# Retention and a maxout layer in one kernel: the values of a tile's four blocks put into one insertion

## The chip, the cores and the metric

The kernel runs on one core of a Trainium2 chip. The metric is the device time of one execution in microseconds (us); lower is better. The tensor engine is called PE here, VectorE is DVE, ScalarE is ACT, GpSimd is POOL, and SP is the engine that issues nearly all transfers.

## The reference

```python
batch, n_heads, seq, head_dim = (8, 8, 576, 64)
# retention
scores = scale * np.matmul(q, k.transpose(0, 1, 3, 2))
gamma = 1.0 - 2.0 ** (-5.0 - np.arange(H, dtype=np.float32))
rel = pos[:, None] - pos[None, :]
Dmat = np.where(rel >= 0, gamma[:, None, None] ** rel[None, :, :], 0.0)
attn = np.matmul(scores * Dmat[None], v)
x = attn.transpose(0, 2, 1, 3).reshape(B * S, H * D)        # 4608 x 512
# maxout layer, w1, w2, w3: 512 x 768, w_out: 768 x 512
h = np.maximum(np.maximum(x @ w1, x @ w2), x @ w3)
out = h @ w_out
```

All is float32 on the chip; the weights come as 64-bit floats, which the kernel turns into float32 itself.

## The kernel before

**Tiles and chunks.** The 4608 tokens are nine tiles (0 to 8) of 512 tokens; a tile is four chunks (blocks) of 128, called a, b, c, d in `steps`. A chunk of the retention part goes through five steps: `load` and `load_blocks` issue its transfers, `transposes` turns q and k, `decay` scales v (on ACT, one head at a time, handed out by `scale`), `scores` multiplies k by q and makes the state of the next 64 tokens, `values` makes the retention output, which DVE scales into the tile `xT`.

From chunk 8 on (`BY_CHUNKS`) scores and values work on pieces of 64 tokens, in the four 64x64 quarters of PE: `chunk_scores` (L323 scores `sk`, L326 states `kv`) and `chunk_values` (L440, masked scores by v; L447, q by the state). After the scores DVE masks them (L330, `m`) and one or two `keep_chunk` steps add the new state to the old (L338, into a buffer `s`); where the state belongs to the next chunk POOL scales it (L340). After the values DVE makes two outputs for each pair of chunks (`xT<-o,gq`, shown at L209), and with the last pair 13 sums of columns of x (`sums_of_x`).

**The layer.** `ffn(t)` is the layer of tile t. From tile 1 on, the three products x @ w are made by a scheme with fewer multiplications on sums of blocks: `up` has 20 products for each of three groups of hidden columns, each of two matmuls of 256 columns (L816), with copies from PSUM on ACT (L801) and joins on DVE (L804). `downs` (tiles 2 to 8) makes the output by 20 products more (L661) into chains E, G, I, H, C, F, D, with copies on ACT (L650) and sums on DVE (L484). One of these sums, `u = C + k7` after product 15, reads the PSUM bank of chain C, on which product 19 goes on adding. Tile 1 uses another scheme for the output (`downs_seven`), tile 0 plain products.

**How the two are woven.** While the layer of tile t runs, the retention part of tile t + 1 is made in between, at twelve places: `steps(t + 1)` is a list of what is done at each, and `ffn(t)` yields at these places. Places 0 to 8 lie one ninth of the 120 matmuls of `up` apart (after matmul 14, 27, 40, 54, 67, 80, 94 and 107), place 9 at their end, 10 behind the fourth product of `downs`, 11 behind the tenth. What is put in between on PE at a place is called an insertion.

DVE steps and loads are not done at their place but put in a queue, `urgent`, by `soon`. Within `up`, one is taken every four matmuls (one more when over six wait); `scores` and `values` empty the queue first. In the last products two are taken per product. Other DVE sums (`chores`) take the remaining turns. ACT scalings are taken one per three matmuls, and all at the next scores. [...]

**Buffers.** `part` tiles (11) hold copies, states, transposed q of the first chunks and other short-lived data. Transposed q has the tag m1 (3 buffers), transposed k the tag kT (2), masked scores the tag m0 (2). States share 4 buffers (tag s), v 4, `xT` 2. The PSUM pool `ps_r` has four banks: scores of two chunks take all four, the values of a pair take two.

## Time and profile before

| what | value |
| --- | --- |
| median of three runs | 744.47 us (743.42 to 744.48) |
| the profiled execution | 744.55 us, its span 742.0 us |
| PE / PE weight loads / DVE / ACT / POOL busy | 735.4 / 607.4 / 578.2 / 336.2 / 36.6 us |
| scores, 64x64 (L323 and L326), records | 896 and 784 |
| values, 64x64 (L440 and L447), records | 896 and 800 |
| outputs `xT<-o,gq`, 128x512 (L209) | 28, 683 ns each |
| transposes on DVE, 128x512 (L209), k and q | 26 of 704 ns, 26 of 692 ns |
| 64-partition state sums (L338) / masks (L330) | 43 of 689 ns / 28 of 687 ns |
| granted PE clock | 1.00 |

The profile comes from one execution. Starts and durations are in us from the start of its span. PE's matmuls overlap one another, so their durations add up to more than the time they take; starts tell the rate. One float32 matmul of the program leaves two records.

### The profile page before, as it was taken

To read this page: it belongs to the slowest core of one execution; us is meant where nothing else is said; L and a number is where in the kernel's file an instruction comes from. 1 tells how busy PE (TensorE), PEld (TensorE's weight loads), DVE (VectorE), ACT (ScalarE), POOL (GpSimd) and SP (SyncE) were. 2 spreads that over 40 slices of the span, in tenths; PEclk is the share of its full clock that TensorE was granted. 3 is DMA by queue.
4 is the path that set the end of the run, shared out by engine and by line. 5 is a ranking of instruction groups with operands and counts; after the bars stand their busy time and mean duration, and the time that the engine had idled before them with its cause. 6 is when DMAs were issued, how large, how long until landed. Compare 5 with 4: busy or idle time off the path is not lost.

```text
span 742.0 us, 16834 instructions
## 1 busy us (share of the span) xinstructions
PE 735.4 (99%) x6716; PEld 607.4 (82%) x6716; DVE 578.2 (78%) x1061; ACT 336.2 (45%) x693; POOL 36.6 (5%) x42
## 2 busy tenths in 40 slices
PE   8999999999999999999999999999999999999998
PEld 6645546888888888888888888888888888888887
DVE  4998899999886895698668876788768956893676
ACT  4764533454255434544355425543455255424441
POOL 2000000022000100000000001000100010000000
PEclk9999999999999999999999999999999999999999
DMA  9996842505242505241424243232514150000001
GB/s 217 241 244 142 227 94 77 96 14 96 66 84 43 103 31 103 41 82 44 109 55 71 45 100 73 45 71 49 122 25 92 42 114 18 1 31 29 0 1 57
DMA packets 230493, 59.30 MB, mean 80 GB/s; under 512 B 211216, under 2 KB 229136, under 8 KB 230416
## 3 DMA queue, kind: packets, MB, share of 16 engines
q1 hardware_dynamic: 229152, 57.98, 36.1%
q8 instruction: 52, 0.85, 0.5%
q10 hardware_dynamic: 1264, 0.27, 0.2%
q14 instruction: 25, 0.20, 0.1%
HBM read 48.76 MB, written 9.44 MB: 78 GB/s over the span
## 4 chain that ended last, share of the span: by engine, by line
PE 97%; DMA 2%; SPq 0%; DVE 0%; issue 0%
PE a L816 20%; PE b L816 17%; PE c L816 9%; PE up L841 9%; PE di L661 7%; PE d L816 6%; PE e L816 6%; PE dhc L661 5%; PE deg L661 3%; PE sk L323 3%; PE down L828 3%; PE o L440 2%; PE dfd L661 2%; PE o L447 2%; DMA qraw<-in_q_dram 1%; PE dx L568 1%
## 5 line engine op out<-in xcount | busy, mean ns | idle before, releaser
L804 DVE TENSOR_TENSOR part<-part 128x512 f32<-128x512 f32 x168 | 117.9, 702 | 86.6 <-ACT part L801 84.0
L801 ACT COPY part<-b 128x512 f32<-128x512 f32 x120 | 70.2, 585 | 164.1 <-PE b L816 162.1
L804 DVE TENSOR_TENSOR h<-h,part 128x512 f32<-128x512 f32 x120 | 83.3, 694 | 24.3 <-ACT h L801 19.8
L801 ACT COPY part<-a 128x512 f32<-128x512 f32 x96 | 56.2, 585 | 52.1 <-PE a L816 51.6
L816 PE MATMUL b<-s,n 128*128 128x256 f32 x288 | 73.9, 379 | 0.0
L204 ACT ACTIVATE vraw<-vraw,gk 128x64 f32<-128x64 f32 x208 | 67.6, 347 | 0.2 <-DMA vraw<-in_v_dram 0.2
L841 PE MATMUL up<-xT,w 128*128 128x512 f32 (+2 forms) x160 | 64.1, 554 | 0.0
L816 PEld LDWEIGHTS b<-s,n 128*128 128x128 f32 x288 | 54.7, 190 | 7.4
L841 PEld LDWEIGHTS up<-xT,w 128*128 128x128 f32 x160 | 28.5, 190 | 30.1 <-issue 26.7
L816 PE MATMUL c<-xT,w 128*128 128x256 f32 x192 | 51.3, 389 | 0.0
L816 PE MATMUL d<-s,w 128*128 128x256 f32 x192 | 49.8, 380 | 0.0
L650 ACT COPY k<-di 128x256 f32<-128x256 f32 x49 | 18.2, 372 | 68.5 <-PE di L661 43.5
L816 PE MATMUL a<-s,w 128*128 128x256 f32 x192 | 49.3, 379 | 0.0
L816 PE MATMUL a<-xT,w 128*128 128x256 f32 x192 | 49.3, 379 | 0.0
L816 PE MATMUL b<-xT,n 128*128 128x256 f32 x192 | 49.3, 379 | 0.0
L340 POOL TENSOR_TENSOR s<-s,gs_of 64x512 f32<-64x512 f32 x21 | 22.5, 1070 | 489.9 <-DVE s L338 438.0
L816 PE MATMUL a<-xT,n 128*128 128x256 f32 x192 | 45.4, 379 | 0.0
L816 PE MATMUL e<-xT,w 128*128 128x256 f32 x192 | 45.4, 379 | 0.0
L816 PEld LDWEIGHTS e<-xT,w 128*128 128x128 f32 x192 | 36.5, 190 | 5.4 <-issue 0.5
L816 PEld LDWEIGHTS a<-xT,n 128*128 128x128 f32 x192 | 36.5, 190 | 5.0
L816 PEld LDWEIGHTS b<-xT,n 128*128 128x128 f32 x192 | 36.5, 190 | 5.0
L816 PEld LDWEIGHTS a<-xT,w 128*128 128x128 f32 x192 | 36.5, 190 | 5.0
(181 smaller groups left out, 1376.2 us busy)
## 6 DMA issues: line engine op xcount, KB each, us to landing
bits<-in_moe_w_dram SPq DMA_DIRECT2D x36, 256.0 KB, 5.5
kraw<-in_k_dram SPq DMA_DIRECT2D x32, 256.0 KB, 3.1
vraw<-in_v_dram SPq DMA_DIRECT2D x32, 256.0 KB, 3.6
qraw<-in_q_dram SPq DMA_DIRECT2D x224, 32.0 KB, 2.1
kxraw<-in_k_dram SPq DMA_DIRECT2D x224, 32.0 KB, 2.1
out_dram<-osb SPq DMA_DIRECT2D x56, 128.0 KB, 1.7
bits<-in_moe_w_out_dram SPq DMA_DIRECT2D x6, 512.0 KB, 5.4
out_dram<-osb SPq DMA_DIRECT2D x7, 256.0 KB, 2.0
```

Of the source, the lines that this page charges most:

```text
L204: scaling.popleft()()
L323: nc.tensor.matmul(s[half(c), h, :], lhsT=kT[half(c), h, :], rhs=qT[half(c), h, :], start=True, stop=True)
L340: nc.gpsimd.tensor_tensor(new, new, factor, op=ALU.mult)
L440: nc.tensor.matmul(o[m][half(c), n, u, :], lhsT=vds[g][half(m), h, :], rhs=sts[g][half(m), h, :], start=n == 0 and u == 0, stop=place(g, m ...
L447: nc.tensor.matmul(o[m][half(c), n, u, :], lhsT=stacks[g][half(m), h, :], rhs=qks[g]["q"][half(m), h, :], start=False, stop=True, skip_gro ...
L650: nc.scalar.copy(place, a)
L661: nc.tensor.matmul(banks[chain], lhsT=hidden(h, order, b, late_ones)[:, e], rhs=late["V"][v][:, e], start=begins and e == 0, stop=chain no ...
L801: nc.scalar.copy(of[step], ps[step[0]][:])
L804: nc.vector.tensor_tensor(of[dst], a, b, op=op)
L816: nc.tensor.matmul(ps[chain][:, e, :], lhsT=factor(w, 2 * fp + e), rhs=xS[t][x], start=n == 1 and e == 0, stop=ends, skip_group_check=True)
L828: nc.tensor.matmul(b[:], lhsT=h[:, fb, m * P:(m + 1) * P], rhs=w_sb["out", fb], start=fb == blocks[0], stop=fb == blocks[-1])
L841: nc.tensor.matmul(ps[:, a:b], lhsT=w_sb[i, fb][:, dc * P:(dc + 1) * P], rhs=xT[t][:, dc, a:b], start=dc == 0 and a == 0, stop=dc == NDC - ...
```

## The change

For tiles 2 to 8 the list of places is written anew. Scores of a and b go to place 4, scores of c and d to place 8 (they were at 1 and 7; for tile 2 at 2 and 7). The values of both pairs go to place 10 (they were at 4 and 10; for tile 2 at 5 and 10). The transposes of a move from place 10 of the tile before to place 0, those of b stay at the tile's start (place 1 instead of 0, or 1 for tile 2), those of c and d go to places 5 and 6. Loads of q and k blocks, of k and of v are asked for separately: blocks at places 2, 3 and 7, k at 4, 9 and 10, v at 10 and 11.

So that four chunks can wait for their values: masked scores are written into the buffer of the transposed k, whose place c and d take in the tag m0; transposed q gets four buffers and states five. `xT` has one buffer instead of two, and that of tile 0 lies in a pool that is closed after tile 0. The part buffers are seven from the start and four more in the pool that opens late in tile 0; from then on a count goes round all eleven.

```diff
-PARTS = 11
+PARTS, LATE_PARTS = 7, 4
-    vpool = ctx.enter_context(tc.tile_pool(name="vpool", bufs=4))
+    vpool = ctx.enter_context(tc.tile_pool(name="vpool", bufs=5))
-    xpool = ctx.enter_context(tc.tile_pool(name="xpool", bufs=2))
+    xpool = ctx.enter_context(tc.tile_pool(name="xpool", bufs=1))
+    late, parts_made = {}, []
+    def part(shape, name):
+        pool, bufs = ppool, PARTS
+        if "N" in late:
+            if len(parts_made) % (PARTS + LATE_PARTS) >= PARTS:
+                pool, bufs = late["pool"], LATE_PARTS
+            parts_made.append(name)
+        return pool.tile(shape, FP32, tag="part", name=name, bufs=bufs)
...
     def load(g, names="kqv"):
-        if g >= BY_PE and ("q", g) not in raws:
+        if g >= BY_PE and "q" in names and ("q", g) not in raws:
...
-                t = vpool.tile([C, H, D], FP32, tag="v", name="vraw")
+                t = vpool.tile([C, H, D], FP32, tag="v", name="vraw", bufs=4)
...
         if g >= BY_CHUNKS:
-            for n, tag in (("k", "kT"), ("q", "m1")):
-                both[n] = att.tile([P, H, D], FP32, tag=tag, name=n + "T", bufs=2 if n == "k" else 3)
+            for n, tag, bufs in (("k", "kT" if g % CPT < 2 else "m0", 2), ("q", "m1", 4)):
+                both[n] = att.tile([P, H, D], FP32, tag=tag, name=n + "T", bufs=bufs)
...
-        st = sts[g] = att.tile([P, H, D], FP32, tag="m0", name="m", bufs=2)
+        st = sts[g] = kT
...
         if i == 0:
-            xT[t] = xpool.tile([P, NDC, NT], FP32, tag="xT", name="xT")
+            xT[t] = (xpool if t else raw0).tile([P, NDC, NT], FP32, tag="xT", name="xT")
...
-        for n in range(0, CPT, 2):
-            a, b, m = CPT * t + n, CPT * t + n + 1, 6 * (n // 2)
-            first_pair = a == BY_CHUNKS
-            s = m + 2 if first_pair else m + 1
-            at(m - (n > 0), (transposes, b))
-            if first_pair:
-                at(m, (decay, b), (load, a + 2), (carry, a))
-            at(s, (scores, a), (scores, b), (load, b + 2))
-            at(s + 1, (decay, a + 2))
-            at(s + 2, (decay, b + 2))
-            at(s + 3, (values, [a, b]), (transposes, a + 2), (load, a + 4))
+        first = t * CPT == BY_CHUNKS
+        a, b, c, d, *following = range(CPT * t, CPT * (t + 2))
+        at(0, (decay, b))
+        if first:
+            at(0, (carry, a))
+        else:
+            at(0, (transposes, a), (decay, a))
+        at(1, (transposes, b))
+        at(2, (load, c, "kqv" if first else "q"))
+        at(3, (load, d, "qv" if first else "q"))
+        at(4, (scores, a), (scores, b), (decay, c), (load, d, "k"))
+        at(5, (transposes, c), (decay, d))
+        at(6, (transposes, d))
+        at(7, *((load, g, "q") for g in following[:2]))
+        at(8, (scores, c), (scores, d))
+        at(9, *((load, g, "k") for g in following[:2]))
+        at(10, (values, [a, b]), (values, [c, d]), *((load, g, "v") for g in following[:2]), (load, following[2], "kv"))
+        at(11, (load, following[3], "v"))
         return todo
```

All other uses of the part buffers call `part` with the same shapes as before.

## The prediction, made before the changed kernel was seen to run

> **What bounds the kernel now.** I read the page's busy shares first, then the chain of work that ended last, then who waited for whom on PE, then the order of time of PE and DVE in one tile.

> ```profile
> PE 735.4 (99%) x6716; PEld 607.4 (82%) x6716; DVE 578.2 (78%) x1061; ACT 336.2 (45%) x693; POOL 36.6 (5%) x42
> PE 97%; DMA 2%; SPq 0%; DVE 0%; issue 0%
> PEld o L440 <- issue: 4.6, 14, 0.3
> PEld sk L323 <- issue: 4.0, 12, 0.3
> PEld dhc L661 <- DVE u L484: 1.4, 5, 0.3
> ```

> PE is the chain: 97% of it. So the time moves only if PE has less to do, or begins to wait. The third to fifth lines (us in total, times, longest) are all that PE's weight loads lose steadily: about 0.33 us at the head of each insertion of values (L440) and of scores (L323), and a few short waits for the DVE sum `u`. The cost of an insertion is read in time order (start, duration, group, records):

> ```profile
> 303.89 1.03 PE L816 MATMUL a<-s,w 128*128 128x256 f32 x4
> 304.84 1.16 PE L440 MATMUL o<-m,vraw 64*64 64x64 f32 x64
> 305.83 1.11 PE L447 MATMUL o<-qT,s 64*64 64x64 f32 x64
> 306.87 1.13 PE L816 MATMUL c<-xT,w 128*128 128x256 f32 x4
> 307.84 1.03 PE L816 MATMUL b<-s,n 128*128 128x256 f32 x4
> ...
> 324.44 0.23 PE L323 MATMUL sk<-qT,kT 64*64 64x64 f32 x2
> ...
> 325.20 0.23 PE L323 MATMUL sk<-qT,kT 64*64 64x64 f32 x2
> ...
> 325.26 0.22 PE L323 MATMUL sk<-qT,kT 64*64 64x64 f32 x2
> ...
> 326.19 0.23 PE L323 MATMUL sk<-qT,kT 64*64 64x64 f32 x2
> ```

> A product of two 256-column matmuls is four records and takes 0.865 us from start to start. From 303.89 to 307.84 are 3.95 us, two of them products: the insertion costs 3.95 - 2 x 0.865 = **2.22 us**. The four-quadrant stream itself runs at one group of four 64-column records per 0.0583 us (324.44 to 326.19 is 30 groups); 128 records are 32 groups, 1.87 us. So **0.355 us** of each insertion is edge: 0.09 before its first matmul, 0.05 ramp on the second group, 0.11 behind the last, 0.10 on the product that follows. The last lines also show what a seam within one insertion costs: 325.20 to 325.26 is the step from chunk c to chunk d, the usual 0.06.

> [...]I use starts, not durations (a product shows 1.03 but takes 0.865). [...]edges appear where 128x128 meets 64x64, and none where a chunk ends. [...]one such sum takes 1.12 us instead of 0.69 just when POOL scales a state (DVE, 330.54). I use that below.

> **The change on PE.** Products, scores, values: same matmuls. Scores stay two insertions a tile, at places 4 and 8 instead of 1 and 7. Values go from two insertions to one. `steps` works this way for tiles 2 to 8, that is during tiles 1 to 7: seven insertions fewer. If the seam between the two pairs is as free as in scores: 7 x 0.355 = **2.49 us saved**. The unseen thing is that seam, where PE meets two other PSUM banks. Bounds: nothing saved[...] to all of it; I take all, by the seam of scores.

> **The change on DVE, where cover could go.** Tile 3, with its last products from 337.69 (call it D):

> ```profile
> 333.74 0.68 DVE L338 TENSOR_TENSOR s<-kv,s 64x512 f32<-64x512 f32 x1
> 335.91 2.15 DVE L804 TENSOR_TENSOR part<-part 128x512 f32<-128x512 f32 x3 [1.50 <-ACT part L801]
> ...
> 353.47 0.70 DVE L209 STREAM_TRANSPOSE kT<-kxraw 128x512 f32<-128x512 f32 x1
> 354.10 0.39 DVE L484 TENSOR_TENSOR osb<-deg,k 128x256 f32<-128x256 f32 x1
> 354.41 0.69 DVE L209 STREAM_TRANSPOSE qT<-qraw 128x512 f32<-128x512 f32 x1
> 355.03 0.38 DVE L484 TENSOR_TENSOR u<-dhc,k 128x256 f32<-128x256 f32 x1
> 355.46 1.13 PE L661 MATMUL dhc<-w_out,h 128*128 128x256 f32 x4
> ```

> DVE has its last idle time (1.50) before 335.91 and then works without a gap; its sum `u` reads the bank of chain C, which the matmul at 355.46 goes on filling. `u` ends at 355.41: **slack 0.05 us**. The 1.13 instead of 1.03 is a weight load that came late, 0.10 us for PE. This is the point where DVE sets PE, tile by tile.

> Now the same stretch after. Scores of c and d come 13 matmuls (5.62 us) later and end at 331.98 on this tile's clock. Chunk c's mask and two keeps and d's mask are 4 x 0.72, plus 0.43 for POOL: from 331.0 to about 334.3, before the join at 335.91, inside DVE's idle time that these same operations leave earlier. Chunk d's two keeps are popped one per four matmuls, behind that join: + 2 x 0.70 = 1.40, and 0.43 if POOL's scaling of the second collides. The outputs of a and b join those of c and d: + 2 x 0.60 = 1.20. The transposes of the next tile's first chunk leave, to place 0: - 0.63 - 0.62 = -1.25 (353.47 to 354.10, 354.41 to 355.03). Sum + 1.35 to + 1.78. But PE also gets to its matmul later, as the second pair's values, 1.87, now lie before it. New slack: 0.05 + 1.87 - 1.78 to 1.35 = **0.1 to 0.6 us**. So no added wait, and the five late weight loads (5 x 0.10) may go: 0 to 0.5 gained; I count nothing. In tile 7 no transposes leave, but its slack before is over 1 us.

> **Other waits, costed at nothing, and their cover.** Chunk d's second keep ends about 341.9 and frees the bank that the second pair's values take at 337.69 + 3.46 + 0.09 + 1.92 = 343.2: cover 1.3. The ten sums of hidden columns before the late products start up to 1.8 later, the products behind the insertion 1.87 later. Masks in place of keys wait for the same scores as before. One x buffer: its writer comes after the last product that reads it. Part buffers are still 11 once the late pool is open; before, seven, and each reuse I followed waits for a chunk two or more back. State buffers: five, for a to d and the next a. ACT: 16 scalings have 53 matmuls before place 8, one per three, so 17 slots; none is left for the last products. SP: a q and k block load is 16 issues, about 0.49 each, 7.9 us; two of them now start at place 7 and end near D + 4, before the first output at D + 10. Blocks of c are loaded three places (17.3 us) ahead of their transposes instead of six: 17.3 - 1.7 - 7.9 - 2.1 landing leaves 5. Values' inputs are issued behind the twelfth product, some 5 us before ACT wants them, landing 3.6. In tile 1 the first seven-form product wants a joined half 1.7 us after its start, and a keep now stands ahead of that join: 0 to 0.3 us, once.

> **The sum.** The profiled execution took 744.55 (span 742.0, 2.5 around it); the median of the three runs is 744.47, which is the same. 744.5 - 2.5 = 742.0.

> **Rivals.**
> 1. *Slower: DVE becomes late at `u`.* Six tiles (2 to 7) have this point. Behind the slack of 0.1 to 0.6, each us DVE is late costs PE one. It eats the gain when DVE is 0.42 + 0.35 = 0.8 us later a tile than worked out, and is slower by over 0.2% when 4 us are lost, 0.67 a tile beyond slack. Two DVE operations more behind the join at 335.91 do it (say d's mask and a keep of c pushed past it): 1.4 - 0.35 = 1.05 a tile, 6.3 in all: 748. For it: DVE is at 19.1 of 19.6 us in this stretch. Against: the idle 1.50 us before it.
> 2. *Same: [...]* The second pair waits for its banks, or restarts as an insertion does: saving 0 to 0.7, 744.1. Against: the seam of scores, and the 1.3 us cover.
> 3. *Faster still: the late weight loads go as well:* 741.4.
> 4. *The order is not what I read*, some blocks land late and DVE stands behind a transpose: 0.5 a tile, 743 to 746.

> **How the numbers follow.** A measurement of this kernel can tell about 0.2%, 1.5 us, from no change: faster is below 743.0. Forecast 0.58, third rival 0.12: faster 0.70. Second rival and the mild half of the fourth: 0.13. First rival and the rest of the fourth: 0.17. The range goes from the third rival, less 0.3, to the mild end of the first: 741.1 to 745.5; what it leaves out is DVE late by more than 0.8 us beyond slack.

> **What would show it.** Seven insertions of up to 256 values records, each near 4.09 us against 2 x 2.22; the L440 heads from 14 to 7; scores at matmul 54 and 107 of a tile. A PEld wait for `u` over 0.3 us a tile, or a gap between the pairs, would make it wrong.

## The result and the profile after

The changed kernel took **751.26 us** (median; 750.61 to 751.85) against 744.47: ratio 1.0095 with a 95% interval of 1.008 to 1.011. It is slower by 6.8 us; 742.0 was forecast. Line numbers are 11 higher from here on. The page's busy shares and the chain of work that ended last, of the changed kernel:

```profile
span 748.8 us, 16773 instructions
PE 736.0 (98%) x6716; PEld 607.9 (81%) x6716; DVE 581.1 (78%) x1061; ACT 336.1 (45%) x693; POOL 35.4 (5%) x42
PE 92%; DVE 4%; issue 1%; DMA 1%; ACT 1%; SPq 0%; ACTq 0%; DVEq 0%
```

PE does the same 6716 matmul records, but it is only 92% of the chain, where it was 97%. Who waited for whom (us in total, times, longest), the lines that matter:

```profile
ACT vraw L215 <- DMA vraw<-in_v_dram: 19.3, 6, 4.0
PEld o L458 <- issue: 4.0, 4, 1.2
PEld o L451 <- issue: 2.6, 5, 1.2
PEld b L827 <- ACT part L812: 1.5, 1, 1.5
```

The values (L451 and L458) have 9 waits that are put down to no releaser ("issue") instead of 14, but of up to 1.2 us instead of 0.33. In order of time, the insertion of tile 6's values (made during tile 5), and two lines of that of tile 4's:

```profile
499.53 1.16 PE L451 MATMUL o<-kT,vraw 64*64 64x64 f32 x64
500.51 1.11 PE L458 MATMUL o<-qT,s 64*64 64x64 f32 x64
501.44 1.11 PE L451 MATMUL o<-kT,vraw 64*64 64x64 f32 x64
502.38 0.34 PE L458 MATMUL o<-qT,s 64*64 64x64 f32 x9
503.77 1.04 PE L458 MATMUL o<-qT,s 64*64 64x64 f32 x39 [1.06 <-issue]
...
344.18 0.41 PE L451 MATMUL o<-kT,vraw 64*64 64x64 f32 x14
344.95 0.97 PE L451 MATMUL o<-kT,vraw 64*64 64x64 f32 x50 [0.37 <-issue]
```

The seam between the pairs (500.51 to 501.44: 16 groups in 0.93) is free, as forecast. But the stream breaks behind record 201, in the middle of one operation; in the last two lines behind record 142. Over the seven insertions it breaks at records 208, 177, 142, 235, 201, 166 and 132, for 1.21, 1.07, 0.58, 0.77, 1.27, 1.26 and 0.32 us from start to start: 6.5 us, against 2.49 of edges saved. The position has nothing to do with chunks or operations. From tile to tile it moves by 31 to 35 records, or those less 128. The page's third part hints at why:

```profile
q8 instruction: 52, 0.85, 0.5%
```

52 pieces of instructions, 0.85 MB: 16 KB each. PE ran 2 x 6716 = 13432 instructions (a weight load and a matmul per record); 13432 / 52 is 258. Counted by their starts in this trace, with 71 of PE's sequencer, 3009, 4546, 6081, 7873, 9410, 10945 and 12482 instructions of PE stand ahead of the seven breaks: steps of 1535 to 1537 and one of 1792, which are 6 and 7 times 256, give or take one. So 256 instructions, 128 records, is the estimate for a piece that is used from here on. In each of the seven a piece of instructions has landed 1.20 to 1.57 us before PE goes on. By that estimate a piece lasts 128 x 0.216 = 27.7 us in the products, in the values 128 x 0.0146 = 1.87.

So the theory tested first: **PE eats its instructions faster than they are fetched**, once two block boundaries (the points where PE passes from one piece to the next) fall into one burst. The rival: PE waits in the second pair for a mask, a state or a bank.

### The profile page after: what moved, and what is told of

It reads as the page before. It is cut to its first block, busy times and chain, and to the rows that moved or that the text cites. A ratio compares the mean times of both kernels' runs of the same rounds, so it can differ in the third digit from the quotient of the medians.

```text
span 748.8 us, 16773 instructions
## 1 busy us (share of the span) xinstructions
PE 736.0 (98%) x6716; PEld 607.9 (81%) x6716; DVE 581.1 (78%) x1061; ACT 336.1 (45%) x693; POOL 35.4 (5%) x42
## 4 chain that ended last, share of the span: by engine, by line
PE 92%; DVE 4%; issue 1%; DMA 1%; ACT 1%; SPq 0%; ACTq 0%; DVEq 0%
PE a L827 19%; PE b L827 16%; PE up L852 8%; PE c L827 8%; PE d L827 6%; PE di L672 6%; PE e L827 5%; PE dhc L672 4%; PE sk L334 3%; PE down L839 3%; PE deg L672 3%; PE dfd L672 2%; PE dx L579 1%; PE o L451 1%; PE o L458 1%; PE s L312 1%
## 5 line engine op out<-in xcount | busy, mean ns | idle before, releaser
L815 DVE TENSOR_TENSOR h<-h,part 128x512 f32<-128x512 f32 x120 | 85.3, 711 | 24.3 <-ACT h L812 20.4
L215 ACT ACTIVATE vraw<-vraw,gk 128x64 f32<-128x64 f32 x208 | 71.5, 350 | 19.3 <-DMA vraw<-in_v_dram 19.3
L661 ACT COPY k<-di 128x256 f32<-128x256 f32 x49 | 18.2, 372 | 98.2 <-PE di L672 88.7
L351 POOL TENSOR_TENSOR s<-s,gs_of 64x512 f32<-64x512 f32 x21 | 24.3, 1159 | 461.2 <-DVE s L349 453.9
L827 PEld LDWEIGHTS a<-s,w 128*128 128x128 f32 x192 | 36.5, 190 | 5.0
```

Source lines behind the costliest of these rows:

```text
L215: scaling.popleft()()
L351: nc.gpsimd.tensor_tensor(new, new, factor, op=ALU.mult)
L661: nc.scalar.copy(place, a)
L815: nc.vector.tensor_tensor(of[dst], a, b, op=op)
L827: nc.tensor.matmul(ps[chain][:, e, :], lhsT=factor(w, 2 * fp + e), rhs=xS[t][x], start=n == 1 and e == 0, stop=ends, skip_group_check=True)
```

## The experiments

Each ratio is taken against runs of the kernel before on the same chip, whose medians there are 744.3 to 745.4 us. A run goes by the number of its paragraph.

**1. Move the blocks, and nothing else.**

```diff
-    warm(6)
+    warm(22)
```

> The changed kernel with 16 more warm-up matmuls at the start: 64 more PE instructions (32 matmul records) ahead of everything, nothing else. Theory 1 (PE runs out of fetched instructions; blocks of 256 instructions, that is 128 matmul records): the pauses in the seven insertions of values stay about 1 us long but move 32 records earlier, or 96 later where that leaves the insertion: from records 208, 177, 142, 235, 201, 166, 132 to about 176, 145, 238, 203, 169, 134, 228. Theory 2 (PE waits in the second pair for a mask, a state or a PSUM bank): the records stay where they are. Time under both: some 4 us more at the start.

Measured: the breaks are at records 176, 145, 238, 203, 169, 134 and 228, all as forecast; 753.23 us (one run). The insertion shown above, in this run, breaks at record 64 + 64 + 41 = 169 instead of 201:

```profile
504.16 0.80 PE L451 MATMUL o<-kT,vraw 64*64 64x64 f32 x41
506.45 0.52 PE L451 MATMUL o<-kT,vraw 64*64 64x64 f32 x20 [1.49 <-issue]
```

No data, order or buffer of the values changed, only the count of instructions before them (64 more). The rival falls.

**2. The burst alone, in the kernel before.**

```diff
-        for n, g in enumerate(chunks):
...
+        for _ in range(2):
+            for n, g in enumerate(chunks):
...
```

> The kernel before, with the matmuls of each pair's values issued twice in a row (the same values computed again): 14 insertions of 256 records, all data ready for the second pass, DVE with more slack than before. Theory 1: the second pass costs 1.87 us and a pause near 1 us in most insertions, also at place 4: 744.5 + 14 x 2.8 = 783. Theory 2: no pause in any of them: 744.5 + 14 x 1.87 = 770.7.

Measured: 785.2 us (one run), and a break in 12 of the 14 insertions, at place 4 as well as in the last products. So no other part of the change is needed for it. Of the two without a break, one holds a single boundary; in the other the piece landed 1.55 us before the second boundary.

**3. One product between the pairs.**

```diff
-        at(10, (values, [a, b]), (values, [c, d]), ...)
+        at(10, (values, [a, b]))
+        at(11, (values, [c, d]), ...)
...
-                chore(4)
+                chore(5)
...
-                if n in (1, 3):
+                if n in (1, 2):
...
-                if n in (3, 9):
+                if n in (3, 4):
```

> The changed kernel with one product of the output between the two pairs' values (in tile 1 one product of six matmuls), and five DVE chores per product in tile 1 instead of four. Theory 1: a product of 0.865 us gives the fetch that much more time, so a pause of 1.0 becomes 0.1 to 0.3, and an edge of 0.355 comes back: 7 x (0.87 - 0.36) = 3.6 us less, about 747.5. Theory 2: the wait shrinks likewise, so this run alone does not tell; it gives the dose.

Measured: no break within the values of any tile; one of 1.3 us right behind the last. But 751.15, ratio 1.0081 (1.0066 to 1.0096), not 747.5. The 108 records of products ahead of tile 2's first scores took 28.1 us instead of 23.4 (24.8 in the changed kernel): 3.0 of it is a wait for ACT (see run 5), most of the rest a slower PE behind it (granted clock 0.51 from 208.3 to 211.4; see the last section). So the breaks fell as expected and the time did not.

**4. Two bursts again: the first pair at place 9.**

```diff
-        at(9, *((load, g, "k") for g in following[:2]))
-        at(10, (values, [a, b]), (values, [c, d]), ...)
+        at(9, (values, [a, b]), *((load, g, "k") for g in following[:2]))
+        at(10, (values, [c, d]), ...)
```

> The changed kernel with the values of a and b at place 9, before the last products; those of c and d stay at place 10. Theory 1: no insertion has over 128 records of values, no pause: 6.5 us back, about 0.9 just behind the last insertion and about 1 us of DVE waits at the last products back, 2.5 us of edges lost: 745.4. Theory 2: the second pair starts only 0.3 us later after its scores than in the changed kernel, so its wait stays, about 0.8 each: near 751.

Measured: no break anywhere, but 749.39, ratio 1.0056 (1.0039 to 1.0073): 4 us over the forecast. Here is what the breaks had covered up to then. First the DVE sum `y14` (`osb<-dhc,k`) of the kernel before and of this one, in tile 3, then PE's product 15 in this one:

```profile
351.01 0.42 DVE L484 TENSOR_TENSOR osb<-dhc,k 128x256 f32<-128x256 f32 x1
```

```profile
356.15 0.42 DVE L495 TENSOR_TENSOR osb<-dhc,k 128x256 f32<-128x256 f32 x1
...
356.62 1.13 PE L672 MATMUL dhc<-v,h 128*128 128x256 f32 x4 [0.58 <-DVE osb L495]
```

Product 15 is the first of chain C and takes the bank from which `y14` reads chain H. Before, `y14` ended at D + 13.74 and the product began at D + 14.31. Here D, the end of `up`, is 339.35, and the first pair's values follow it: `y14` ends at D + 17.22, 3.48 later, while the product is only 2.22 later. PE loses 0.75 and a late weight load of 0.1 in each of tiles 2 to 5: 3.4 us. The other 2 us are the wait at the start of tile 2.

**5. Loads of v early.** In the changed kernel, ACT and PE at the start of tile 2:

```profile
206.48 0.35 ACT L215 ACTIVATE vraw<-vraw,gk 128x64 f32<-128x64 f32 x1 [3.95 <-DMA vraw<-in_v_dram]
...
207.35 1.13 PE L827 MATMUL b<-s,w 128*128 128x256 f32 x4 [1.13 <-ACT part L812]
```

ACT's first scaling waits 3.95 us for a load of v, and ACT's copies of PE's results, which PE needs to have its banks free, stand behind it (the first starts at 206.74).

```diff
-        at(10, (values, [a, b]), (values, [c, d]), *((load, g, "v") for g in following[:2]), ...)
+        at(10, (values, [a, b]), *((load, g, "v") for g in following[:2]), (values, [c, d]), ...)
```

> The changed kernel with the next tile's first two loads of v issued right behind the first pair's values instead of behind the sums of x. If the wait of 1.5 us at the start of tile 2 comes from ACT standing behind a load of v (its copies follow in the same queue), it goes and nothing else does: ratio 1.0095 less 0.0018, about 1.0077. If it comes from something else (the sums of x, DVE), it stays, and the ratio stays at 1.0095. The pauses in the values stay either way.

Measured: the wait is gone, and the first 108 records of tile 2's `up` take 23.40 us as elsewhere. Yet 752.65, ratio 1.0102 (1.0078 to 1.0125), no less than the changed kernel: during tiles 4 to 6 the insertions take 5.81, 6.02 and 5.42 us instead of 4.76, 5.21 and 5.15, while the loads now pass beside them, and behind one of them the granted clock was 0.53 from 425.6 to 429.2 (see the last section). In the first two of these the piece landed 2.67 and 2.53 us behind the burst's first boundary, instead of 1.65 and 1.98, while 0.5 MB of other transfers passed instead of less than 0.1. That the loads hold up the fetch is not shown: one execution does not separate it from chance, and run 6 has a break of 1.70 us with no other transfer beside it.

**6. Scores of c and d back at place 7.**

```diff
-        at(7, *((load, g, "q") for g in following[:2]))
-        at(8, (scores, c), (scores, d))
+        at(7, (scores, c), (scores, d))
+        at(7, *((load, g, "q") for g in following[:2]))
```

> The changed kernel with the scores of c and d at place 7, as before the change, instead of 8. If the waits of PE around the last products (a join in tile 1, the copy k14 in tile 3, some of those at u) come from the keeps that now stand among the joins, they go: about 1 us less, ratio 1.008. The pauses stay, since no PE instruction is added or taken away. If DVE was late for another reason, no difference.

Measured: the waits for DVE in the last products are gone in all tiles, but 765.22, ratio 1.0275 (1.0251 to 1.03). The waits of PE at these scores:

```profile
PEld sk L334 <- DVE qT L220: 10.7, 6, 2.0
```

The transposes of d, asked for at place 6, stand in DVE's queue behind joins and hidden sums and are now needed 13 matmuls sooner. So the change's place 8 for the scores goes with its place 6 for the transposes. With the first pair at place 9 and v early besides, the same wait stays:

> The changed kernel with the values of a and b at place 9, scores of c and d at place 7, and the loads of v early. If starved bursts, late keeps and late v are all that the change lost, nothing is left but the 14 insertions of before: ratio 0.998 to 1.001, no pause, no wait for u (the first pair's values now lie before the last products and give DVE 2.2 us). If buffers or the order of loads cost something besides, it stays above 1.002.

Measured: 756.27, ratio 1.015 (1.0134 to 1.0167); no break, no wait in the last products or at the start of tile 2, only the 10.7 us at the scores. A miss of the forecast for that one reason.

**7. The transposes earlier too.** As the last one, and:

```diff
-        at(4, ..., (decay, c), (load, d, "k"))
-        at(5, (transposes, c), (decay, d))
-        at(6, (transposes, d))
+        at(4, ..., (decay, c), (decay, d), (load, d, "k"), (transposes, c))
+        at(5, (transposes, d))
-                if step % 4 == 1 or step % 4 == 3 and len(urgent) > (2 if t == 1 else 6):
+                if step % 4 == 1 or step % 4 == 3 and len(urgent) > (2 if t == 1 else 0):
```

> As the run with all three repairs (values of a and b at place 9, scores of c and d at place 7, v early), with the transposes of c asked for at place 4 and those of d at 5, and from tile 2 on one queued step every two matmuls instead of four. If the waits of 1.5 to 2 us of those scores came only from d's late transposes, they go, and what is left is the work of before in 14 insertions without the short waits at u: ratio 0.998 to 1.001. If the order of the loads holds the transposes up instead, the waits stay: 1.008 or more.

Measured: **742.94** against 744.29 on its chip, ratio **0.9981 (0.9974 to 0.9988)**: faster than both kernels, by little. Tile 3 in order of time:

```profile
335.82 1.16 PE L451 MATMUL o<-kT,vraw 64*64 64x64 f32 x64
336.80 1.11 PE L458 MATMUL o<-qT,s 64*64 64x64 f32 x64
337.84 1.13 PE L672 MATMUL di<-w_out,h 128*128 128x256 f32 x4
...
341.49 1.16 PE L451 MATMUL o<-kT,vraw 64*64 64x64 f32 x64
342.48 1.11 PE L458 MATMUL o<-qT,s 64*64 64x64 f32 x48
343.52 1.13 PE L672 MATMUL dfd<-w_out,hn 128*128 128x256 f32 x4
```

Two insertions, each with its edges, as before the change; nothing else on PE in tiles 2 to 7 is late, nor the weight loads at `u`. Which of the repairs carries how much of this was not taken apart.

**8. The first pair at place 9 and v early, scores left at place 8.**

> As the run with the values of a and b at place 9, with the loads of v early and the scores of c and d left at place 8. The wait of 2 us at the start of tile 2 goes (1.9 us), the waits for u of about 0.9 us in tiles 2 to 5 stay: ratio 1.0056 - 0.0025 = 1.003.

Measured: 746.48, ratio 1.0028 (1.0017 to 1.0039), as forecast; the four waits at product 15 (4.0 us in PE's weight loads, 3.4 between PE's starts) are most of what stays.

**9. One merged insertion that does not starve.**

```diff
-    warm(6)
+    warm(17)
```

> The changed kernel with 11 more warm-up matmuls at the start, which moves every block boundary 22 matmul records earlier within the insertions. For tile 3's step that puts one boundary 8 records ahead of the merged values, one at record 120, one 8 records behind, each over 3.4 us from the last. Theory 1: this insertion alone has no pause and takes 3.9 us from its first matmul to the next product, 0.36 less than two insertions; the others pause at about records 186, 155, 213, 179, 144 and 238. Theory 2: it pauses like the rest.

Measured: the breaks are at records 186, 155, none, 213, 179, 144 and 238 (753.26 us, one run). The insertion made during tile 3, and a later product of that tile:

```profile
344.56 1.16 PE L451 MATMUL o<-kT,vraw 64*64 64x64 f32 x64
345.54 1.11 PE L458 MATMUL o<-qT,s 64*64 64x64 f32 x64
346.47 1.11 PE L451 MATMUL o<-kT,vraw 64*64 64x64 f32 x64
347.41 1.11 PE L458 MATMUL o<-qT,s 64*64 64x64 f32 x48
348.45 1.13 PE L672 MATMUL dfd<-w_out,hn 128*128 128x256 f32 x4
...
357.81 1.13 PE L672 MATMUL dhc<-v,h 128*128 128x256 f32 x4 [0.47 <-DVE osb L495]
```

From 344.56 to 348.45 are 3.89 us; with the edges of 0.09 and 0.10 at its two ends that is 4.08, and 4.09 was forecast. But in this tile, without the break, product 15 waits for `y14`: 0.63, and 0.1 for a late weight load, more than the 0.355 gained. So even with instructions at hand the change loses in this tile.

## Why the prediction was wrong

- **Edges and seam: right.** 0.355 us an edge, a free seam, 3.89 us where nothing else interfered (run 9).
- **The stream at 0.0583 us a group, "same matmuls": this step failed.** The rate was read from insertions of at most 128 records and used for up to 256. The sum has no term for the supply of instructions, and that term is 6.5 us from start to start. In the kernel before no insertion was long enough to show it.
- **"This is the point where DVE sets PE" (u): the wrong point.** `y14` comes before it, with 0.57 of slack, and before the transposes that leave: the 1.25 us credited for them come too late. The keeps (1.45), the outputs (1.20) and one join beside POOL's scaling of a state (1.42 instead of 0.69, as at 342.87 in the changed kernel: 0.72, taken as 0 to 0.43) make 3.37 of the measured 3.48. That was run 4; in tile 3 of the changed kernel `y14` ends at D + 17.21 (355.46, with D at 338.25), as late. Without a break the slack would have been, as an estimate, 0.57 + 1.87 - 3.48 = -1.04; in run 9, where a wait of 0.47 for `k14` comes before it, PE waits 0.63. In the changed kernel the breaks hide most of it: waits in the last products grow only from 0.6 to 1.4 us. The first rival was right that DVE becomes late, with another sum as its place, but that is at most 0.8 of the 6.8 us: the main loss was in none of the rivals, and the second, which looked for a gap at the seam, had its place wrong.
- **"Values' inputs are issued behind the twelfth product": not in tile 1**, which has other last products and takes four queued steps in each of seven. There the loads of v are issued from 200.5 us on, the tile ends at 201.75, and ACT waited 3.95 us: 1.4 us on PE.
- **Part buffers: a cover too thin.** The copy k14 in tile 3 waits for a part buffer that a join, now behind a keep, lets go: 0.47 us.
- The join in tile 1 cost 0.24 us, within the 0 to 0.3 forecast.
- Two small sums slip, and nothing rests on them: 17.3 - 1.7 - 7.9 - 2.1 leaves 5.6, not 5, and the third rival is 742.0 - 0.5 = 741.5, not 741.4.

On PE: - 2.49 edges; + 6.8 breaks with the slow restarts behind them (each insertion less 3.89); + 0.85 a wait in the second product behind the last insertion, where the next boundary lies; + 1.4 tile 2; + 0.8 last products; - 0.5 in the time before tile 1's products, not looked into. The sum is 6.9; the two profiles lie 6.8 apart.

## What to carry to other kernels

The rate measured in bursts of up to 128 records, 0.0583 us a group of four, wasn't that of bursts of 240 and 256, which broke for 0.32 to 1.27 us: count the instructions, not only the data, and look how fast they arrive. If a gap moves as instructions are added far ahead of it, look to supply and not to a dependency: in run 1, 64 more moved every break 32 records earlier or 96 later, with no dependency changed. And when one stall is taken away, list every reader of every bank in order, with its slack: a credit, here of 1.25 us, counts only for waits that come after it.

## What the runs showed of the hardware that was not expected

Behind two of PE's stops the profile shows a lower granted clock. In run 5, in the stretch behind the break during tile 4, in which PE stood idle for 1.60 us (columns: stretch; busy us and count of PE, PEld, DVE, ACT, POOL; granted clock; DMA share; GB/s):

```profile
425.60:429.20 3.60, 3.60 (x10) 2.87 (x9) 3.57 (x9) 0.00 (x0) 0.00 (x0) 0.53 0.02 5
429.30:440.00 10.70, 10.70 (x51) 9.43 (x50) 8.32 (x23) 2.85 (x8) 0.00 (x0) 1.00 0.37 101
```

From 426.85 to 428.56 four records start, 0.427 us apart instead of 0.216. In run 3 the granted clock was 0.51 from 208.3 to 211.4 us, after PE had waited 3.0 us, and 1.00 from there on. In the changed kernel, with breaks of up to 1.27 us, it was 1.00 throughout. What it takes to lower the clock is not shown.
